# A spectral mixing layer and two MLPs on one core: Fourier phases staggered on every queue, transfers reordered

## The chip, the cores and the metric

The kernel runs on one core of a Trainium2 chip. A core has TensorE (PE: matmuls, weight loads shown as PEld), VectorE (DVE), ScalarE (ACT), GpSimd (POOL) and SyncE (SP), each with its own queue of instructions worked off in order, and 16 DMA engines, to which here SP and ACT issue. PE writes its results to PSUM, from which DVE and ACT read them. The metric is the device time of one execution in microseconds (us).

## The reference

```python
def _attn_ref(x, w_r, w_i, b_r, b_i):          # x: (2, 3008, 256)
    X = np.fft.rfft(x, axis=1)
    Yr = Xr @ w_r - Xi @ w_i + b_r
    Yi = Xr @ w_i + Xi @ w_r + b_i
    Yr = np.sign(Yr) * np.maximum(np.abs(Yr) - 0.01, 0.0)      # Yi alike
    return np.fft.irfft(Yr + 1j * Yi, n=3008, axis=1)

x = attn_out.reshape(6016, 256)
h = x @ w_in                                   # (256, 2048), float64 weights
x = (np.maximum(h, 0.0) + alpha * np.minimum(h, 0.0)) @ w_out
h = x @ w_in2
g = where(h >= 1, h, where(h <= -1, 0, (h + 1) ** 2 / 4))
return g @ w_out2
```

## The kernel before

The sequence of 3008 points is a product of 47 and 64. The Fourier transform is done in two matmul stages with a trip through DRAM between them, the inverse likewise.

- `f1` (L216): one of 16 x groups (8 for each of the two batches), the 47-point stage: 4 fp32 matmuls (the trace counts 8), results copied from two PSUM tiles by ACT (L224) and DVE (L226) to `ae`, stored to `a_dr` in two halves (`store_a`), and read back transposed (`load_a`) into `a_sb`.
- The second stage runs over 24 items (12 pairs of frequencies for each batch). For an item j, `f2` (L296) makes the spectrum (`psf`), ACT writes its rounded part fh (L305) and a negated third of it (L307), DVE the remainder fl (L306). `mix` (L310) first lets ACT negate a third of fl (L312); then PE runs 26 matmuls with the complex weights `wm` (L316, L321 to L323; L323 reads fl), and DVE applies the threshold (clip L326, y L327). `split_y` splits y into yh (ACT, L334) and yl (POOL, L335). `i1` (L338) is the 64-point inverse stage, 6 matmuls to `psi`, copied by ACT to ve (L346) and stored to `v_dr`.
- `p3` (L360) is the 47-point inverse stage for one of 16 groups: loads of v from `v_dr`, 8 matmuls (L367; 16 in the trace), copied by ACT (L371) and DVE (L373) to `y`.
- The MLPs run over 2 layers, 12 chunks of up to 512 rows and 16 blocks f of 128 hidden units: `first` (matmuls to `psh`, L421 and L422 on DVE make ta), `late` (gh on ACT L405, gl on POOL or, for odd f of the first chunk, DVE, L406) and `second` three steps behind.
- The float64 weights are split into two float32 parts on the core: `convert_w` in four parts over ACT (L143, L144, L159), DVE (L145, L171, L156, L161) and POOL (L162, L164, L165); the buffers cm and cp are two deep. The generator `conversions` gives one step at each `next(conv, None)`: a light step (parts 3 and 1, and two DMA issues on ACT for a weight block two ahead) and a heavy one (parts 2 and 0) take turns, 35 in all for the first layer.

The order on each queue is the order in which the code is written (a manual schedule). One turn of the loop (L461 to L487) writes, for item j: f2 of j + 2, an f1 of batch 1 (j < 5), split_y of j - 1, mix of j, some transfers, split_n (j < 6; it splits the constants of the inverse stage), p3 from j = 16, i1 of j - 2 with its copy, and a conversion step. PSUM has two tags, h and o, with four buffers each. The p3 of batch 1 stand in the second MLP chunk.

Of the kernel before, what the change touches and what calls it, by code (L numbers as in the profile page):

```python
# [79 lines left out]
def spectral_mlp_kernel(ctx: ExitStack, tc: tile.TileContext, x, w_r, w_i, bias, c_e, c_f1, c_f2,  # L80
# [159 lines left out]
    def load_m(k):  # L240
        nc.sync.dma_start(m_t[k].rearrange("p k f -> p (k f)"), c_f2[:, 1024 * k:1024 * (k + 1)])
# [54 lines left out]
    def f2(b, i):  # L296
        ps = psum.tile([128, 4, 128], F32, tag="h", name=f"psf{b}_{i}")
        for k in range(2):
            for c in range(2):
# [4 lines left out]
        xl = piece([128, 4, 192], F32R, f"fl{b}_{i}")
        A.activation(xh[:, :, 64:192], ps, AF.Copy)  # L305
        V.tensor_tensor(xl[:, :, 64:192], ps, xh[:, :, 64:192].bitcast(F32), op=ALU.subtract)  # L306
        A.mul(xh[:, :, 0:64], xh[:, :, 128:192].bitcast(F32), -1.0)  # L307
        xt[b, i] = xh, xl

    def mix(b, i):  # L310
        xh, xl = xt.pop((b, i))
        A.mul(xl[:, :, 0:64], xl[:, :, 128:192].bitcast(F32), -1.0)  # L312
        ps = psum.tile([128, 2, D], F32, tag="o", name=f"psm{b}_{i}")
        for k in range(2):
            o = ps[:, k, :]
            T.matmul(o, e_t, b_t, start=True, stop=False)  # L316
            for c in range(2):
                j = 2 * k + c
                for r, off in ((0, 64), (1, 0)):
# [40 lines left out]
    def p3(g):  # L360
# [36 lines left out]
    def late(step):  # L397

        if step is None:
            return  # L400
        l, c, f = step
        ps, gh, gl, ta, tb = gt[step]
        if l == 1:
            V.tensor_tensor(ta, ps, tb, op=ALU.max)  # L404
        A.activation(gh, ta, AF.Copy)  # L405
        (V if (l, c) == (0, 0) and f % 2 else G).tensor_tensor(gl, ta, gh.bitcast(F32), op=ALU.subtract)  # L406

    def first(l, c, f, before):
# [81 lines left out]
    DEPTH = 3  # L490
    seq = [(l, c, f) for l in range(2) for c in range(NC) for f in range(NF)]
    for i in range(len(seq) + DEPTH):
        if i < len(seq):
# [57 lines left out]
```

## Time and profile before

| | us |
|---|---|
| median of 3 runs (lowest, highest) | 1300.51 (1299.91, 1305.77) |
| the profiled execution | 1304.99 |
| its span, first to last instruction | 1303.2 |
| PE busy | 1235.4 (95%) |
| DVE, ACT, POOL busy | 702.3, 528.7, 656.8 |

The share of busy PE time is an average over a Fourier part of some 235 us and the MLPs behind it. A matmul's end is modelled, so its start, and the start of the next, say more than its length. The rows that the prediction uses stand below.

### The profile page before, as it was taken

Reading aid. Unit: us, or ns where it says so; the run is one execution under the profiler, and the core shown is the slowest. Engines: PE = TensorE matmul, PEld = TensorE weight load, DVE = VectorE, ACT = ScalarE, POOL = GpSimd, SP = SyncE. Lnnn points to the kernel's source line nnn. Section 1 sums busy time; section 2 is a strip of 40 time slices with the busy share of each in tenths; the row PEclk is TensorE's granted clock in tenths of the full one; section 3 lists DMA queues with packets and bytes.
Section 4 is the critical chain, followed back from the end, with each engine's and each line's share of the span. In section 5 each row is a group of like instructions: output and inputs, shape, how many; then the busy total and the mean of one; then the engine's idle time right before and its main releaser. Section 6 shows DMA issues by size and latency. Waiting matters only on the chain.

```text
span 1303.2 us, 16032 instructions
## 1 busy us (share of the span) xinstructions
PE 1235.4 (95%) x5958; PEld 1046.6 (80%) x5958; DVE 702.3 (54%) x1034; ACT 528.7 (41%) x905; POOL 656.8 (50%) x512
## 2 busy tenths in 40 slices
PE   8687777979999999999999999999999999999998
PEld 6676777758888889888888898888888988888887
DVE  1443334885566666655555576455545554555453
ACT  1344444433233333332222235454544454445544
POOL 0014533773577777765444468444444444444444
PEclk8898999989999999999999999999999999999999
DMA  9953333503001010000000010000000000000000
GB/s 264 303 169 114 89 114 89 145 17 97 18 17 33 17 33 17 18 1 1 1 1 1 1 65 1 17 17 1 17 17 17 1 15 17 17 1 17 17 17 15
DMA packets 37181, 59.38 MB, mean 46 GB/s; under 512 B 3248, under 2 KB 25328, under 8 KB 37104
## 3 DMA queue, kind: packets, MB, share of 16 engines
q1 hardware_dynamic: 22016, 39.08, 9.3%
q10 hardware_dynamic: 15088, 19.28, 5.0%
q8 instruction: 46, 0.75, 0.2%
q14 instruction: 31, 0.25, 0.1%
HBM read 39.61 MB, written 18.74 MB: 45 GB/s over the span
## 4 chain that ended last, share of the span: by engine, by line
PE 87%; ACT 4%; DVE 3%; DMA 3%; POOL 1%; issue 1%; ACTq 1%; SPq 0%; DVEq 0%; POOLq 0%
PE psh L99 13%; PE psh L100 13%; PE pso L100 13%; PE psh L101 13%; PE pso L99 13%; PE pso L101 13%; PE ps L367 2%; PE psm L323 2%; PE psm L322 2%; PE psm L321 2%; DMA x<-in_x 1%; PE ps L222 1%; ACT yh L334 1%; ACT fh L305 1%; DMA a_dr<-ae 1%
## 5 line engine op out<-in xcount | busy, mean ns | idle before, releaser
L406 POOL TENSOR_TENSOR gl<-ta,gh 128x512 fp32r<-128x512 f32 (+1 forms) x376 | 485.0, 1292 | 444.6 <-ACT gh L405 443.6
L405 ACT ACTIVATE gh<-ta 128x512 fp32r<-128x512 f32 (+1 forms) x384 | 239.0, 622 | 310.5 <-DVE ta L422 302.4
L100 PE MATMUL pso<-gl,w 128*128 128x512 f32 (+1 forms) x768 | 299.1, 389 | 7.0 <-DVE gl L406 5.5
L99 PE MATMUL psh<-mxh,w 128*128 128x512 f32 (+1 forms) x768 | 297.9, 388 | 4.1 <-POOL w L165 4.1
L100 PE MATMUL psh<-mxl,w 128*128 128x512 f32 (+1 forms) x768 | 297.6, 388 | 0.0
L99 PE MATMUL pso<-gh,w 128*128 128x512 f32 (+1 forms) x768 | 297.2, 387 | 0.0
L101 PE MATMUL pso<-gh,w 128*128 128x512 f32 (+1 forms) x768 | 296.6, 386 | 0.0
L101 PE MATMUL psh<-mxh,w 128*128 128x512 f32 (+1 forms) x768 | 296.3, 386 | 0.0
L425 DVE TENSOR_SCALAR tb<-psh 128x512 f32<-128x512 f32 (+1 forms) x192 | 130.4, 679 | 233.9 <-PE psh L101 232.7
L421 DVE TENSOR_SCALAR tb<-psh,alpha_t 128x512 f32<-128x512 f32 (+1 forms) x192 | 141.6, 738 | 160.1 <-PE psh L101 159.9
L426 ACT ACTIVATE tb<-tb 128x512 f32<-128x512 f32 (+1 forms) x192 | 119.8, 624 | 262.2 <-DVE tb L425 262.2
L100 PEld LDWEIGHTS pso<-gl,w 128*128 128x128 f32 x768 | 144.7, 188 | 38.2 <-DVE gl L406 7.6
L99 PEld LDWEIGHTS psh<-mxh,w 128*128 128x128 f32 x768 | 144.6, 188 | 33.1 <-POOL w L165 5.0
L99 PEld LDWEIGHTS pso<-gh,w 128*128 128x128 f32 x768 | 144.6, 188 | 28.3
L101 PEld LDWEIGHTS psh<-mxh,w 128*128 128x128 f32 x768 | 144.4, 188 | 28.0
L101 PEld LDWEIGHTS pso<-gh,w 128*128 128x128 f32 x768 | 144.6, 188 | 27.5
L100 PEld LDWEIGHTS psh<-mxl,w 128*128 128x128 f32 x768 | 144.6, 188 | 26.7
L422 DVE SCALAR_TENSOR_TENSOR ta<-psh,tb 128x512 f32<-128x512 f32 (+1 forms) x192 | 130.7, 681 | 20.5 <-POOL gl L406 1.5
L404 DVE TENSOR_TENSOR ta<-psh,tb 128x512 f32<-128x512 f32 (+1 forms) x192 | 128.4, 669 | 0.2 <-ACT tb L426 0.2
L335 POOL TENSOR_TENSOR yl<-y,yh 128x512 fp32r<-128x512 f32 x24 | 31.1, 1297 | 135.2 <-ACT yh L334 119.0
L323 PE MATMUL psm<-wm,fl 128*128 128x256 f32 x192 | 60.4, 314 | 39.5 <-ACT fl L312 39.4
L323 PEld LDWEIGHTS psm<-wm,fl 128*128 128x128 f32 x192 | 40.4, 210 | 44.1 <-ACT fl L312 44.1
(62 smaller groups left out, 1017.8 us busy)
## 6 DMA issues: line engine op xcount, KB each, us to landing
u<-in_w_in ACTq DMA_DIRECT2D x32, 256.0 KB, 3.0
u<-in_w_out ACTq DMA_DIRECT2D x32, 256.0 KB, 3.5
a_dr<-ae SPq DMA_DIRECT2D x32, 192.0 KB, 4.5
v_dr<-ve SPq DMA_DIRECT2D x12, 512.0 KB, 4.7
v<-v_dr SPq DMA_DIRECT2D x16, 384.0 KB, 3.9
x<-in_x SPq DMA_DIRECT2D x15, 384.0 KB, 7.4
out<-yt SPq DMA_DIRECT2D x20, 256.0 KB, 2.1
a<-a_dr SPq DMA_DIRECT2D x6, 768.0 KB, 7.6
```

Of the source, the lines that this page charges most:

```text
L99: T.matmul(ps, wl, xh, start=start, stop=False)
L100: T.matmul(ps, wh, xl, start=False, stop=False)
L101: T.matmul(ps, wh, xh, start=False, stop=stop)
L323: T.matmul(o, xl[:, j, off:off + 128], wm[r][:, 0, c, :], start=False, stop=last)
L335: G.tensor_tensor(yl, y32, yh.bitcast(F32), op=ALU.subtract)
L404: V.tensor_tensor(ta, ps, tb, op=ALU.max)
L405: A.activation(gh, ta, AF.Copy)
L406: (V if (l, c) == (0, 0) and f % 2 else G).tensor_tensor(gl, ta, gh.bitcast(F32), op=ALU.subtract)
L421: V.tensor_scalar(tb, ps, 0.0, alpha_t[:, f:f + 1], op0=ALU.min, op1=ALU.mult)
L422: V.scalar_tensor_tensor(ta, ps, 0.0, tb, op0=ALU.max, op1=ALU.add)
L425: V.tensor_scalar(tb, ps, 1.0, -1.0, op0=ALU.min, op1=ALU.max)
L426: A.activation(tb, tb, AF.Square, bias=0.5, scale=0.5)
```

## The change

The change moves instructions and transfers; the arithmetic and the number of instructions stay the same on each engine.

- In an item's turn of the loop the negation of fl is a function of its own (`negate_low`) and is written for item j + 1; the threshold (`threshold`) of item j - 1 comes behind the f2 of j + 2 and right ahead of split_y; the copy of i1 (`evict_i1`) comes one turn later, behind split_y; p3 comes ahead of the mix.
- f1 and p3 take both PSUM tiles from tag h.
- Conversion steps begin at item 5 (before: 3), and even items from 10 on take two: 26 steps in the items, before 21.
- The p3 of batch 1 move from the second MLP chunk to steps 8 to 15 of the first. In layer 0, late() works on the step's own block, not on the one before.
- Transfers: m is loaded in halves, the constants n one by one from SP (before: all three on ACT, early), w_r and w_i from SP behind x group 9 (before: early on ACT), x groups 8 to 15 and the pieces of a in another order.

```diff
@@ -217,7 +217,7 @@
-            ps = psum.tile([96, 2, D], F32, tag="h" if i else "o", name=f"ps1_{b}_{j}_{i}")
+            ps = psum.tile([96, 2, D], F32, tag="h", name=f"ps1_{b}_{j}_{i}")
...
-    load_m(0)
-    wm32 = [rot.tile([128, 2, D], F32, tag="tb", name=f"wm32_{k}") for k in range(2)]
-    A.dma_start(wm32[0], w_r.rearrange("(c p) e -> p c e", p=128))
-    A.dma_start(wm32[1], w_i.rearrange("(c p) e -> p c e", p=128))
...
-        if g in (3, 5, 7):
-            load_x(8 + (g - 3) // 2)
+        if g == 5:
+            load_m(0, 0)
+        if g == 6:
+            load_x(8)
     load_a(0, A_PARTS[:2])
+    load_x(9)
+    for k, w in enumerate((w_r, w_i)):
+        nc.sync.dma_start(wm32[k], w.rearrange("(c p) e -> p c e", p=128))
     for g in range(8):
         store_a(g, 1)
+    load_x(10)
+    load_m(0, 1)
     load_a(0, A_PARTS[2:3])
-    load_x(11)
-    load_m(1)
-    load_a(0, A_PARTS[3:])
-    load_x(12)
     f1(8)
-    load_x(13)
     f1(9)
-    n32 = [rot.tile([128, 8, 128], F32, tag="wst", bufs=3, name=f"n32_{k}") for k in range(3)]
-    for k in range(3):
-        A.dma_start(n32[k].rearrange("p k f -> p (k f)"), c_i1[:, 1024 * k:1024 * (k + 1)])
...
         A.activation(xh[:, :, 64:192], ps, AF.Copy)
+        A.mul(xh[:, :, 0:64], xh[:, :, 128:192].bitcast(F32), -1.0)
         V.tensor_tensor(xl[:, :, 64:192], ps, xh[:, :, 64:192].bitcast(F32), op=ALU.subtract)
-        A.mul(xh[:, :, 0:64], xh[:, :, 128:192].bitcast(F32), -1.0)
         xt[b, i] = xh, xl
+
+    def negate_low(b, i):
+        xl = xt[b, i][1]
+        A.mul(xl[:, :, 0:64], xl[:, :, 128:192].bitcast(F32), -1.0)
...
-        late(before)
+        late((l, c, f) if l == 0 else before if before[0] == 1 else None)
...
     f1(10)
-    load_x(14)
-    for g in range(8, 11):
-        store_a(g, 0)
-        store_a(g, 1)
-    load_x(15)
     f2(*items[1])
+    negate_low(*items[0])
+    for k, g in ((0, 11), (1, 12)):
+        store_a(8 + k, 0)
+        store_a(8 + k, 1)
+        load_x(g)
+    load_a(0, A_PARTS[3:4])
+    load_n(0)
+    store_a(10, 0)
+    store_a(10, 1)
+    load_m(1, 0)
     for j in range(n):
         if j + 2 < n:
             f2(*items[j + 2])
+        if j >= 1:
+            threshold(*items[j - 1])
+            split_y(*items[j - 1])
+        if j >= 3:
+            evict_i1(*items[j - 3])
+        if j + 1 < n:
+            negate_low(*items[j + 1])
         if j < 5:
             f1(11 + j)
-        if j >= 1:
-            split_y(*items[j - 1])
+        if 14 <= j < 17:
+            load_v(j - 14)
+        if j >= 16:
+            p3(j - 16)
         mix(*items[j])
...
-        if j >= 3:
+        if j >= 5:
             next(conv, None)
+        if j >= 10 and j % 2 == 0:
+            next(conv, None)
...
-        if (l, c) == (0, 1) and i < len(seq) and f % 2 == 1:
-            p3(8 + f // 2)
+        if (l, c) == (0, 0) and f >= 8:
+            p3(f)
```

ACT's queue in the turn of item 8 of batch 0. Names as above; the first number in a name is the item. Before:

```order
L305 ACTIVATE fh_10_830<-psf_10_825 128x4x128
L307 ACTIVATE fh_10_830<-fh_10_830 128x4x64
L334 ACTIVATE yh_7_835<-y_0_7_805 128x512
L312 ACTIVATE fl_8_703<-fl_8_703 128x4x64
L346 ACTIVATE ve_6_879<-psi_6_872 128x512
L159 ACTIVATE w_1_881<-cm_1_757 128x512
L143 ACTIVATE cm_2_885<-u_2_694 128x512
L144 ACTIVATE u_2_694<-u_2_694 128x512
```

After:

```order
L307 ACTIVATE fh_10_812<-psf_10_807 128x4x128
L308 ACTIVATE fh_10_812<-fh_10_812 128x4x64
L343 ACTIVATE yh_7_821<-y_0_7_818 128x512
L358 ACTIVATE ve_4_764<-psi_5_795 128x512
L314 ACTIVATE fl_9_752<-fl_9_752 128x4x64
L159 ACTIVATE w_0_863<-cm_0_741 128x512
L143 ACTIVATE cm_1_867<-u_1_682 128x512
L144 ACTIVATE u_1_682<-u_1_682 128x512
```

The negation in this turn is that of item 9, not 8, and the copy to ve that of the inverse of item 5, not 6.

DVE's queue in the same turn. Before:

```order
L306 TENSOR_TENSOR fl_10_831<-psf_10_825,fh_10_830 128x4x128
L326 TENSOR_SCALAR clip_8_867<-psm_8_840 128x512
L327 TENSOR_TENSOR y_0_8_868<-psm_8_840,clip_8_867 128x512
L161 TENSOR_SCALAR cp_1_758<-cm_1_757 128x512
L145 TENSOR_SCALAR cp_2_886<-u_2_694 128x512
```

After:

```order
L309 TENSOR_TENSOR fl_10_813<-psf_10_807,fh_10_812 128x4x128
L335 TENSOR_SCALAR clip_7_817<-psm_7_767 128x512
L336 TENSOR_TENSOR y_0_7_818<-psm_7_767,clip_7_817 128x512
L161 TENSOR_SCALAR cp_0_742<-cm_0_741 128x512
L145 TENSOR_SCALAR cp_1_868<-u_1_682 128x512
```

Between the two fl the threshold is now that of the item before, whose y the yh of the same turn reads.

DVE's queue in the first MLP chunk, steps 6 and 7. Before:

```order
L421 TENSOR_SCALAR tb_0_6_2128<-psh_0_6_2118,alpha_t 128x512
L422 SCALAR_TENSOR_TENSOR ta_0_6_2127<-psh_0_6_2118,tb_0_6_2128 128x512
L406 TENSOR_TENSOR gl_0_5_2098<-ta_0_5_2099,gh_0_5_2097 128x512
L161 TENSOR_SCALAR cp_12_2080<-cm_12_2079 128x512
L145 TENSOR_SCALAR cp_13_2138<-u_13_2049 128x512
L421 TENSOR_SCALAR tb_0_7_2158<-psh_0_7_2148,alpha_t 128x512
L422 SCALAR_TENSOR_TENSOR ta_0_7_2157<-psh_0_7_2148,tb_0_7_2158 128x512
L171 TENSOR_SCALAR cm_13_2137<-cm_13_2137 128x512
L156 SCALAR_TENSOR_TENSOR cm_13_2137<-cm_13_2137,cp_13_2138 128x512
```

After:

```order
L432 TENSOR_SCALAR tb_0_6_2171<-psh_0_6_2161,alpha_t 128x512
L433 SCALAR_TENSOR_TENSOR ta_0_6_2170<-psh_0_6_2161,tb_0_6_2171 128x512
L171 TENSOR_SCALAR cm_15_2150<-cm_15_2150 128x512
L156 SCALAR_TENSOR_TENSOR cm_15_2150<-cm_15_2150,cp_15_2151 128x512
L432 TENSOR_SCALAR tb_0_7_2196<-psh_0_7_2186,alpha_t 128x512
L433 SCALAR_TENSOR_TENSOR ta_0_7_2195<-psh_0_7_2186,tb_0_7_2196 128x512
L417 TENSOR_TENSOR gl_0_7_2194<-ta_0_7_2195,gh_0_7_2193 128x512
L161 TENSOR_SCALAR cp_15_2151<-cm_15_2150 128x512
```

An odd step's gl stands in the step itself, behind its ta, and the conversions are two to three weight blocks further on.

## Rows read from the trace of the kernel before

**Rows 1.** The page's slices: busy tenths of PE in 40 equal slices.
```profile
PE   8687777979999999999999999999999999999998
```
**Rows 2.** PE's waits, 60:233: who waited for whom; total us, times, longest.
```profile
PE psm L323 <- ACT fl L312: 39.4, 20, 3.0
```
**Rows 3.** Timeline, ACT and DVE, 121:131: start, length, instruction [idle before].
```profile
121.24 0.48 ACTq L133 DMA_DIRECT2D u<-in_w_out  x1
...
127.55 0.63 ACT L159 ACTIVATE w<-cm 128x512 fp32r<-128x512 f32 x1
...
129.19 0.58 ACT L305 ACTIVATE fh<-psf 128x512 fp32r<-128x512 f32 x1
129.80 0.69 DVE L306 TENSOR_TENSOR fl<-psf,fh 128x512 fp32r<-128x512 f32 x1 [1.29 <-ACT fh L305]
130.12 0.61 ACT L334 ACTIVATE yh<-y 128x512 fp32r<-128x512 f32 x1
130.64 0.40 ACT L312 ACTIVATE fl<-fl 128x256 fp32r<-128x256 f32 x1
```
**Rows 4.** Timeline, DVE: clips of items 0, 4 and 23, and y of 23.
```profile
52.92 0.69 DVE L326 TENSOR_SCALAR clip<-psm 128x512 f32<-128x512 f32 x1 [3.23 <-PE psm L323]
...
79.71 0.69 DVE L326 TENSOR_SCALAR clip<-psm 128x512 f32<-128x512 f32 x1 [3.15 <-PE psm L323]
...
232.41 0.69 DVE L326 TENSOR_SCALAR clip<-psm 128x512 f32<-128x512 f32 x1 [6.76 <-PE psm L323]
233.20 0.69 DVE L327 TENSOR_TENSOR y<-psm,clip 128x512 f32<-128x512 f32 x1
```
**Rows 5.** Timeline, PE: one item with a p3.
```profile
199.15 1.05 PE L300 MATMUL psf<-m,a 128*128 128x128 f32 x8
199.96 0.36 PE L316 MATMUL psm<-b_t,e_t 128*128 128x256 f32 x1
...
202.28 0.38 PE L323 MATMUL psm<-wm,fl 128*128 128x256 f32 x1 [1.37 <-ACT fl L312]
...
204.74 1.95 PE L367 MATMUL ps<-g,v 96*128 96x128 f32 x16
206.45 0.36 PE L99 MATMUL psi<-yh,n 128*128 128x256 f32 x1
```
**Rows 6.** Start: PE timeline (four f1; group 11); window (PE, PEld, DVE, ACT, POOL; PEclk, DMA share, GB/s).
```profile
14.62 7.12 PE L222 MATMUL ps<-x,c 96*96 96x256 f32 x32 [0.35 <-DMA x<-in_x]
...
45.26 3.70 PE L222 MATMUL ps<-x,c 96*96 96x256 f32 x8 [10.04 <-DMA x<-in_x]
...
20.00:40.00 20.00, 13.39 (x57) 9.47 (x55) 7.60 (x14) 6.03 (x12) 0.00 (x0) 0.83 0.98 327
```
**Rows 7.** Timeline, POOL and ACT: a conversion operation; a wait for POOL's L165.
```profile
132.05 1.29 POOL L164 TENSOR_TENSOR cm<-cm,w 128x512 f32<-128x512 f32 x1
...
244.52 0.68 ACT L143 ACTIVATE cm<-u 128x512 f32<-128x512 f32 x1 [1.90 <-POOL w L165]
```
**Rows 8.** The page's DMA issues: count, KB each, us to landing.
```profile
v_dr<-ve SPq DMA_DIRECT2D x12, 512.0 KB, 4.7
v<-v_dr SPq DMA_DIRECT2D x16, 384.0 KB, 3.9
```
**Rows 9.** Timeline, DVE: first step of chunks 0, 1, 2 (L421); two L171.
```profile
236.37 0.75 DVE L421 TENSOR_SCALAR tb<-psh,alpha_t 128x512 f32<-128x512 f32 x1 [0.57 <-PE psh L101]
...
239.84 0.42 DVE L171 TENSOR_SCALAR cm<-cm 128x512 f32<-128x512 f32 x1
...
254.13 1.40 DVE L171 TENSOR_SCALAR cm<-cm 128x512 f32<-128x512 f32 x1
...
294.79 0.75 DVE L421 TENSOR_SCALAR tb<-psh,alpha_t 128x512 f32<-128x512 f32 x1 [2.32 <-PE psh L101]
...
352.86 0.75 DVE L421 TENSOR_SCALAR tb<-psh,alpha_t 128x512 f32<-128x512 f32 x1 [0.83 <-PE psh L101]
```
**Rows 10.** Window over most items with p3, columns as in rows 6.
```profile
162.00:233.00 71.00, 55.90 (x424) 54.28 (x423) 27.52 (x47) 28.01 (x56) 26.33 (x21) 0.92 0.31 93
```

More of the change, by code (lines that the diff above doesn't have):

```diff
@@ L238, in store_a, with load_m @@
         nc.sync.dma_start(a_dr[b][h][4 * j:4 * j + 4].rearrange("t p f -> p t f"), aes[g][48 * h:48 * h + 48])
-    def load_m(k):
-        nc.sync.dma_start(m_t[k].rearrange("p k f -> p (k f)"), c_f2[:, 1024 * k:1024 * (k + 1)])
+    def load_m(k, half):
+        nc.sync.dma_start(m_t[k][:, 4 * half:4 * half + 4, :].rearrange("p k f -> p (k f)"),
+                          c_f2[:, 1024 * k + 512 * half:1024 * k + 512 * half + 512])
     for g in range(8):
@@ L257, in spectral_mlp_kernel @@
     A.dma_start(b32, bias)
+    A.dma_start(alpha_t, alpha)
+    wm32 = [rot.tile([128, 2, D], F32, tag="tb", name=f"wm32_{k}") for k in range(2)]
     for g in range(8):
@@ L285, in spectral_mlp_kernel, with load_n @@
         V.tensor_tensor(b_t[p:p + 32, :], b32[p:p + 32, :], b_t[p:p + 32, :].bitcast(F32), op=ALU.subtract)
+    n32 = [rot.tile([128, 8, 128], F32, tag="wst", bufs=3, name=f"n32_{k}") for k in range(3)]
+    def load_n(k):
+        nc.sync.dma_start(n32[k].rearrange("p k f -> p (k f)"), c_i1[:, 1024 * k:1024 * (k + 1)])
     n_h = []
@@ L323, in mix, with threshold @@
                     T.matmul(o, xl[:, j, off:off + 128], wm[r][:, 0, c, :], start=False, stop=last)
+        y_32[b, i] = ps
+    def threshold(b, i):
+        ps = y_32[b, i]
         cl_ = rot.tile([128, 2, D], F32, tag="ta", name=f"clip{b}_{i}")
@@ L339, in i1 @@
         yh, yl = yt.pop((b, i))
-        ps = psum.tile([128, 2, D], F32, tag="o", name=f"psi{b}_{i}")
+        ps = yt[b, i] = psum.tile([128, 2, D], F32, tag="o", name=f"psi{b}_{i}")
         for k in range(2):
@@ L343, in i1, with evict_i1 @@
             mm3(ps[:, k, :], n_h[q][:, 0, r, :], n_h[q][:, 1, r, :], yh[:, k, :], yl[:, k, :], True, True)
+    def evict_i1(b, i):
+        ps = yt.pop((b, i))
         if i % 2 == 0:
@@ L363, in p3 @@
             y[b] = block(f"a{b}", [128, 2, S], F32, f"yt{b}")
-        ps = [psum.tile([128, 4, 128], F32, tag="ho"[c], name=f"ps3_{b}_{j}_{c}") for c in range(2)]
+        ps = [psum.tile([128, 4, 128], F32, tag="h", name=f"ps3_{b}_{j}_{c}") for c in range(2)]
         for c in range(2):
@@ L397, in late @@
     def late(step):
[L399 to L406, printed above, removed]
+        if step is not None:
+            l, c, f = step
+            ps, gh, gl, ta, tb = gt[step]
+            if l == 1:
+                V.tensor_tensor(ta, ps, tb, op=ALU.max)
+            A.activation(gh, ta, AF.Copy)
+            (V if (l, c) == (0, 0) and f % 2 else G).tensor_tensor(gl, ta, gh.bitcast(F32), op=ALU.subtract)
     def first(l, c, f, before):
@@ L463, in spectral_mlp_kernel @@
             f2(*items[j + 2])
+        if j >= 1:
[5 more added lines that the diff above has]
+            negate_low(*items[j + 1])
         if j < 5:
             f1(11 + j)
-        if j >= 1:
-            split_y(*items[j - 1])
+        if 14 <= j < 17:
+            load_v(j - 14)
+        if j >= 16:
+            p3(j - 16)
         mix(*items[j])
+        if j < 3:
+            load_x(13 + j)
         if j < 5:
@@ L471, in spectral_mlp_kernel @@
             store_a(11 + j, 1)
-        if j == 2:
-            load_m(2)
+        if j == 0:
+            load_a(0, A_PARTS[4:])
+            load_m(1, 1)
+        if j == 1:
+            load_n(1)
+        if j == 3:
+            load_m(2, 0)
+            load_n(2)
+        if j == 5:
+            load_m(2, 1)
         if 5 <= j < 10:
@@ L485, in spectral_mlp_kernel @@
             i1(*items[j - 2])
-        if j >= 3:
+        if j >= 5:
             next(conv, None)
+        if j >= 10 and j % 2 == 0:
+            next(conv, None)
+    threshold(*items[n - 1])
     split_y(*items[n - 1])
+    evict_i1(*items[n - 3])
     DEPTH = 3
@@ L505, in spectral_mlp_kernel @@
                 i1(*items[n - 2 + i])
-            if i == 1:
+            if 1 <= i < 3:
+                evict_i1(*items[n - 3 + i])
+            if i == 2:
                 for g in range(8, 8 + len(v_tags[1])):
```

6 lines of the change are left out of this document (removed).

## The prediction

> **What bounds the kernel now.** I read the page's slices first: the reader is to see that TensorE (PE) is at 9 tenths from the tenth slice of 32.6 us on, and at 6 to 8 in eight of the nine before it [rows 1]. So only the first 300 us or so can give much. Next, who PE waits for there: between 60 and 233 us there is one name, the matmul L323 of the mix, behind ScalarE's (ACT) negation L312, 39.4 us in 20 waits [rows 2]. Third, the order of one item, to see why L312 is late: ACT first splits the spectrum of the item two ahead (fh), then yh, then negates, and only afterwards copies the inverse transform (ve) and converts weights [rows 3]. A mix waits for a negation that stands behind a split, the split behind weight conversion, the conversion behind ve, and ve behind the inverse matmuls that follow the mix: a ring around two engines, once per item. Item 4's clip starts at 79.71 us and item 23's at 232.41 [rows 4]: 152.7 us for 19 items, 8.0 each. PE's own work for one item is far less [rows 5]: f2 0.81 (199.15 to 199.96), mix 26 matmuls of 0.117 (21 of them fill 202.28 to 204.74), 3.05; i1 6 of 0.117, 0.70; together 4.56, and 6.27 with the 1.71 of a p3 (204.74 to 206.45). Before 50 us the bound is DMA: PE waits 10.04 us for x group 11 [rows 6], in a stretch whose DMA engines are 98% busy at 327 GB/s.
>
> **The change, part by part.** Every sum is made on the profiled execution (1304.99 us); its difference is then taken off the median, 1300.51.
>
> (1) DMA order. I count the bytes that stand ahead of x group 11 on both queues. Before: 12 x groups of 0.393 MB, 16 stores of 0.197, m 0.524, w_r and w_i 0.524, the a pieces 0 to 11, 1.57, n 1.573, small constants 0.29: 12.35 MB. After: n has gone behind it, half an m in place of a whole one is no saving because both halves are ahead, and two stores of group 8 have come ahead: 11.17 MB. The difference of 1.18 MB at 327 GB/s is 3.6 us, so group 11 starts PE at 41.65 instead of 45.26. From there to item 0's clip I keep the old 7.66 us (45.26 to 52.92, the row of the clip of item 0 [rows 4]), slow matmuls included (3.70 for this group's eight against 7.12 for 32 earlier on [rows 6]), since PE comes out of a wait here again: 49.3. Items 1 to 4 carry an f1 each, 1.78 us (7.12 for four groups [rows 6]); PE alone needs 0.81 + 1.78 + 3.05 = 5.64, and 0.70 more from item 3 on: 23.96 us. The DMA just keeps up: group 15, the last, has 6.3 MB ahead of it behind group 11, 19 us at that rate, and is wanted some 25 us later. Item 4's clip: 73.3 against 79.71, **-6.4 us**. What is late next there is n (0.524 MB ahead of split_n 0, which holds ACT and VectorE, DVE); it lands before ACT's turn for item 2, with some 5 us to spare.
>
> (2) The ring is opened. L312 now stands in the item before its mix, so a mix finds it done; ve is copied one item later; clip and y (L326, L327) have moved behind fl on DVE. What takes the place of the ring is a smaller loop of ACT and DVE alone, because yh now stands behind fh, fl, clip and y of the same item. Its length, start to start [rows 3, 4]: fh to fl 0.61, fl 0.69, clip to y 0.79, y to yh 0.70 (y's length), yh to the next 0.52, ve as much, being a copy of the same size, negation 0.40: 4.2 us. The fl to clip and y to yh steps are not shown by the trace of before, since there the next operation was never queued directly; they lie between these lengths and 0.1 more for a hand-over. Weight conversion comes on top: its heavy step 1.64 (127.55 to 129.19), its light step two DMA issues of about 0.48, half of it hidden under the operation ahead, 0.5. So 5.85 or 4.7, and 6.35 in every second item from 10 on, which takes both. Where the light step is ahead of the heavy one (item 12 in this stretch), the heavy step's L143 needs the buffer that L165 on GpSimd (POOL) gives back in the same item: yl, L164, L165 of 1.3 each (one of them [rows 7]) after yh's 0.61, then 1.1 of ACT work, so 8.3. Such a wait is in the trace, 1.90 us [rows 7]. Items 5 to 13: 6.6 (four DMA issues and a split_n) + 5.3 + 4.7 + 5.85 + 4.7 + 6.35 + 5.85 + 8.3 + 4.7 = 52.35. All of them exceed PE's 4.56, two by little, so the loop sets the end, with PE waiting a little at each mix. From item 4's mix to the loop's first negation 5.8; item 13's period ends 58.2 us after item 4's mix.
>
> Now v: the copy of item 11's ve comes one item later than before, and the load of v for p3(0) stands right behind its store. Store 4.7 and load 3.9 [rows 8] end 8.4 us later, p3 takes 1.71, so mix 16 starts at 10.1, some 3.7 us after its negation. From there each item costs PE 6.27; ACT's loop is 5.1 to 8.3 with 0.4 for p3's copy, about 6.8 in the mean, but it has that wait to catch up, so I take PE: 3.05 + 5 x 6.27 + 2 x 5.46 (the last two have no f2) = 45.3. Sum: 58.2 + 10.1 + 45.3 = 113.6 against 152.7, **-39.1 us**.
>
> (3) To the first MLP step. Before, 3.96 us from the last clip to the first L421 [rows 4, 9], of which one p3, 1.71, now stands ahead of the mix (and is in the sum above): **-1.7 us**.
>
> (4) The first two MLP chunks. Before: 58.4 and 58.1 us (236.37, 294.79, 352.86 [rows 9]). In the second of them PE works through, 8 p3 included, so PE's own time for a chunk is 58.1 - 13.7 = 44.4. In the first, DVE's conversions set the pace over most steps. After, 26 in place of 21 conversion steps lie in the items, so the conversions end with step 8; p3 moves to steps 8 to 15 of the first chunk. First half: 29.2 if DVE's pace stays, 22.2 if PE sets it; second half 22.2 + 13.7; second chunk 44.4. With the old pace 109.5 against 116.5, **-7 us**; to PE's own, -14. The new place of late() costs on this stretch: on odd steps gl on DVE now waits for gh of the same step, about 0.8 each (a copy of yh's size, 0.61 [rows 3], and two hand-overs) for 4 steps, which leaves -3.8. I take -7, the old pace, as the nearest row. Elsewhere in layer 0 late() moves work that PE's matmuls cover.
>
> (5) Two charges. The granted clock averaged 0.92 in 162 to 233 [rows 10]; the levels are 1.2 and 2.4 GHz, so 16% of the time was at the lower one. PE is now the bound there: 8% of some 55 us, **+4**; nought if it stays high, 9 if it falls twice as often. And DVE's L171 took 0.42 in one place and 1.40 in another, where POOL was at work [rows 9]. In items 10 to 23 ten weight blocks go through L171 and L156; with L156 priced alike, at +0.98 each that is at most 19.6 us, at least 0 (ACT's 0.5 to 1.6 of conversion runs beside them). I take **+4**.
>
> The Trainium skill bears on this (SBUF — State Buffer, Who interferes with whom): VectorE in its two-port modes, or with two SBUF inputs, and GpSimd exclude one another for whole instructions, and whichever starts second waits. The pair of L171 durations agrees. By that rule alone, with every such pair of operations colliding, the charge would be 19.6 instead of 4, which is the first rival.
>
> Sum: -6.4 - 39.1 - 1.7 - 7 + 4 + 4 = -46.2. On the median: 1300.5 - 46.2 = **1254 us**.
>
> **The rivals.** *DVE and POOL collide in each denser item*: the conversions hold fl of the next item up. For it: the 1.40 [rows 9], and four POOL operations of 1.3 in an item that takes both steps. Against: fl, clip and y themselves read PSUM and keep 0.69 in every row shown, beside POOL or not. It puts 19.6 for 4, and -3.8 for -7: 1273.
> *The loop is slack and PE alone sets the items*: 10 x 4.56 in place of 58.2, -12.6, and no charge for collisions: 1238. Against it: yh really does stand behind fl, clip and y.
> *The wait only moves*: negations come no earlier, because ACT's queue as a whole is late; items 5 to 23 keep 8.0, and only the start, the step to the MLP and the MLP chunks gain 15, less the charges of 8: 1293, in half of these cases within 0.5% of before.
> *Slower: the clock stays at 1.2 GHz through the items*, since PE still pauses at each mix. PE's own 10 x 4.56 + 7 x 6.27 + 2 x 5.46 = 100.4 us would become 200.8 against 152.7, +48 less 15: about 1334. It decides from two thirds of the time at the lower level on (100.4 x 1.67 = 168 eats all gains); the trace shows 16%.
>
> **How the numbers follow.** Forecast 0.62, collisions 0.18, PE alone 0.09, the wait moves 0.07 (half of it 0.035 within 0.5%), clock 0.04. Range: the low end is the sum without charges and with PE's pace in the first chunk (-54.2 - 7 = -61), 1239; the high end has 19.6, 9 and -3.8 (-22), 1278. It leaves out the slower case, the moved wait and some of both neighbours: 0.2. A measurement of this kernel tells 0.5% (6.5 us) from no change. Faster by more than that: 0.62 + 0.18 + 0.09 + 0.035, 0.93; within 0.03; slower 0.04.
>
> **What would show it.** Right: L312's successor gone from PE's waits in the items; clips 5.5 to 6.3 us apart; yh or POOL's L165 as releasers on ACT and PE; group 11 near 41.7 us; first MLP step near 190. Wrong: clips still 7 to 8 us apart (the wait moved), a granted clock of 0.7 or less over the items, a p3 that waits longer than 4 us for v, or the first chunk still 58 us long.

## The result and the profile after

The changed kernel takes 1252.98 us (median; 1252.85 to 1253.21), the kernel before 1300.49 us in the same comparison: ratio 0.9626, 95% interval 0.9601 to 0.9651. The forecast was 1254.0. The profiled execution of after took 1252.99 us (span 1251.2), that of before 1304.99, so between the two traces 52.0 us have to be found; 4.5 us of that lie in the profiled execution of before, which was that much above its median.

The page's slices, PE's row, and PE's waits from 50 to 192 us (who waited for whom: total us, times, longest). They answer [rows 1, 2]:

```profile
PE   6998998999999999999999999999999999999998
```

```profile
PE psm L321 <- DVE y L336: 5.4, 3, 2.7
PE psm L328 <- ACT fl L314: 1.5, 4, 0.5
...
PE ps L379 <- DMA v<-v_dr: 0.5, 1, 0.5
```

The 39.4 us behind ScalarE's negation are 1.5. L314 is the old L312. PE is at 9 tenths from the eighth slice on, and was so from the tenth.

The clips of items 4 and 23 and the first step of chunks 0, 1 and 2 in after's DVE timeline (start, length, instruction), against [rows 4, 9]; L335 is the old L326, L432 the old L421:

```profile
75.49 0.68 DVE L335 TENSOR_SCALAR clip<-psm 128x512 f32<-128x512 f32 x1
...
191.45 0.69 DVE L335 TENSOR_SCALAR clip<-psm 128x512 f32<-128x512 f32 x1
...
192.78 0.74 DVE L432 TENSOR_SCALAR tb<-psh,alpha_t 128x512 f32<-128x512 f32 x1
...
257.26 0.75 DVE L432 TENSOR_SCALAR tb<-psh,alpha_t 128x512 f32<-128x512 f32 x1 [0.83 <-PE psh L101]
...
300.86 0.75 DVE L432 TENSOR_SCALAR tb<-psh,alpha_t 128x512 f32<-128x512 f32 x1 [1.17 <-PE psh L101]
```

Chunk 2 begins 52.0 us earlier (352.86 to 300.86): the whole difference lies ahead of it. The same marks were read in the trace of every kernel below (the names are those of the experiments). The stages in us, each a difference of two such starts:

| kernel | median | to item 4's clip | items 4 to 23 | to the first MLP step | chunks 0, 1 | chunk 2 begins |
|---|---|---|---|---|---|---|
| before | 1300.49 | 79.7 | 152.7 | 4.0 | 116.5 | 352.9 |
| after | 1252.98 | 75.5 | 116.0 | 1.3 | 108.1 | 300.9 |
| loop_only | 1257.99 | 81.5 | 103.7 | 2.2 | 117.8 | 305.1 |
| old_dma | 1258.80 | 81.2 | 116.0 | 1.3 | 108.4 | 306.9 |
| old_mlp | 1255.11 | 75.5 | 116.0 | 1.3 | 110.4 | 303.2 |
| single | 1254.24 | 78.2 | 107.8 | 2.2 | 113.9 | 302.1 |
| neg_only | 1251.04 | 79.7 | 99.5 | 4.3 | 117.6 | 301.0 |
| neg_back | 1332.61 | 85.8 | 178.9 | 2.2 | 108.4 | 375.3 |
| single_p17 | 1246.98 | 78.0 | 100.1 | 2.2 | 115.2 | 295.4 |
| extra_p17 | 1241.47 | 76.1 | 103.2 | 1.3 | 108.3 | 289.0 |
| old_order | 1243.39 | 74.5 | 105.5 | 3.0 | 109.5 | 292.4 |
| best | 1240.08 | 74.3 | 100.8 | 3.0 | 107.8 | 285.9 |

Two things in the row of after ask for an explanation. Its items take 116.0 us, 12 to 16 us more than in several kernels that contain only a part of the change. And it is one time for a bundle of edits, which does not say which edit did it.

### The profile page after: what moved, and what is told of

Read it like the earlier page. It is cut to its first block, busy times and chain, and to the rows that moved or that the text cites. A ratio compares the mean times of both kernels' runs of the same rounds, so it can differ in the third digit from the quotient of the medians.

```text
span 1251.2 us, 16024 instructions
## 1 busy us (share of the span) xinstructions
PE 1220.5 (98%) x5958; PEld 1038.1 (83%) x5958; DVE 714.9 (57%) x1034; ACT 527.8 (42%) x905; POOL 655.8 (52%) x512
## 3 DMA queue, kind: packets, MB, share of 16 engines
q1 hardware_dynamic: 23424, 41.18, 10.4%
## 4 chain that ended last, share of the span: by engine, by line
PE 86%; DVE 5%; ACT 2%; POOL 2%; DMA 2%; issue 1%; SPq 0%; ACTq 0%; POOLq 0%; DVEq 0%
PE pso L100 13%; PE psh L100 13%; PE psh L99 13%; PE pso L99 13%; PE pso L101 13%; PE psh L101 13%; PE ps L222 2%; DMA x<-in_x 1%; PE ps L379 1%; DVE cm L156 1%; DMA a_dr<-ae 1%; PE psm L326 1%; PE psm L328 1%; PE psm L327 1%; PE psf L302 1%
## 5 line engine op out<-in xcount | busy, mean ns | idle before, releaser
L417 POOL TENSOR_TENSOR gl<-ta,gh 128x512 fp32r<-128x512 f32 (+1 forms) x376 | 478.6, 1274 | 473.0 <-ACT gh L416 457.0
L432 DVE TENSOR_SCALAR tb<-psh,alpha_t 128x512 f32<-128x512 f32 (+1 forms) x192 | 141.6, 737 | 153.7 <-PE psh L101 153.7
L100 PEld LDWEIGHTS pso<-gl,w 128*128 128x128 f32 x768 | 144.2, 188 | 29.3 <-POOL gl L417 2.7
L96 DVE TENSOR_TENSOR mxl<-yt,mxh 128x1024 fp32r<-128x1024 f32 (+1 forms) x24 | 37.7, 1570 | 39.2 <-ACT mxh L93 39.2
L328 PE MATMUL psm<-wm,fl 128*128 128x256 f32 x192 | 56.3, 293 | 1.5 <-ACT fl L314 1.5
```

Source lines behind the costliest of these rows:

```text
L96: V.tensor_tensor(lo, src, hi.bitcast(F32), op=ALU.subtract)
L100: T.matmul(ps, wh, xl, start=False, stop=False)
L432: V.tensor_scalar(tb, ps, 0.0, alpha_t[:, f:f + 1], op0=ALU.min, op1=ALU.mult)
```

## Which edit carries the gain

**The whole new order inside an item, alone (loop_only).** Transfers, conversion steps (one per item from item 3), third phase and `late()` as before; in the loop:

```
+        if j >= 1:
+            threshold(*items[j - 1])
+            split_y(*items[j - 1])
+        if j >= 3:
+            evict_i1(*items[j - 3])
+        if j + 1 < n:
+            negate_low(*items[j + 1])
...
-        if j >= 1:
-            split_y(*items[j - 1])
         mix(*items[j])
```

> The new order inside an item alone (negation, threshold, copy of i1, place of p3, PSUM tags), with the transfers, the conversion steps (one per item from item 3), late() and the p3 of batch 1 as in the kernel before. Theory: the order carries nearly all of the gain, and single steps even let the items run at PE's pace: 150 us between the clips of items 4 and 23 become 103 to 108, start and MLP as before: 1246 to 1254. Rival: the parts add up and the order in the items is only the 34 us by which these items shrank: 1264 to 1268.

Measured: 1257.99 us, ratio 0.9655 [0.9641, 0.9670], between the two ranges. The items take 103.7 us, as the theory has it; the start and the chunks do not gain. So some 43 of the 47.5 us come with the order inside the items, as the prediction's step (2) has it.

**One line of it (neg_only).** The kernel before with the negation moved and nothing else:

```
+    def negate_low(b, i):
+        xl = xt[b, i][1]
+        A.mul(xl[:, :, 0:64], xl[:, :, 128:192].bitcast(F32), -1.0)
...
     def mix(b, i):
         xh, xl = xt.pop((b, i))
-        A.mul(xl[:, :, 0:64], xl[:, :, 128:192].bitcast(F32), -1.0)
...
+    negate_low(*items[0])
     for j in range(n):
         if j + 2 < n:
             f2(*items[j + 2])
+        if j + 1 < n:
+            negate_low(*items[j + 1])
```

> The kernel before with one line moved: the negation of the low part's copy is written one item earlier, ahead of the next item's f2, instead of directly ahead of its own mix; everything else is as before. Theory (the wait of PE on ScalarE's fl, 39.4 us over 20 items, is this line and nothing else): nearly all of the gain of the run with the whole new order in the items, 1258 us there, so 1256 to 1264, and the stretch from item 4's clip to item 23's near 104 us where it was 152.7. Rival (the wait needs the moved line and the new places of the conversion steps together, since ScalarE stays behind them): 1275 to 1290, with PE's wait on fl at 0.8 us per item or more.

Measured: 1251.04 us (1250.26 to 1253.19), ratio 0.9612 [0.9591, 0.9634]: less than forecast by the theory, and no slower than the whole change. Neg_only's window from 80 to 175 us (length; busy us and instructions of PE, PEld, DVE, ACT, POOL; granted clock; DMA share; GB/s), and the clips of items 4 and 23:

```profile
80.00:175.00 95.00, 95.00 (x820) 95.00 (x820) 69.19 (x98) 61.20 (x123) 58.68 (x42) 1.00 0.56 175
```

```profile
79.66 0.69 DVE L329 TENSOR_SCALAR clip<-psm 128x512 f32<-128x512 f32 x1 [1.41 <-PE psm L326]
...
179.14 0.69 DVE L329 TENSOR_SCALAR clip<-psm 128x512 f32<-128x512 f32 x1 [1.90 <-PE psm L326]
```

PE is busy for 95.00 of 95.00 us at the full clock, and each clip waits for PE's last matmul of the mix (L326 there), as it should where PE is the bound. The items take 99.5 us in place of 152.7. All that the rest of the change gains and loses against this kernel cancels by the table: 4.2 us at the start (transfers), 3.0 at the step to the MLP, 9.5 in the chunks, against 16.5 us that after's items take longer.

**The line put back into the changed kernel (neg_back).**

```
-    negate_low(*items[0])
...
-        if j + 1 < n:
-            negate_low(*items[j + 1])
...
+        negate_low(*items[j])
         mix(*items[j])
```

> The changed kernel with that one line put back directly ahead of its own mix; DMA order, conversion steps, late writing of the first layer and the third phase's place stay as changed. Theory: PE waits again near 2.0 us for fl in each item, 20 x 2.0 = 39 us, less what the shorter conversion steps spare, so 1280 to 1294. Rival (the other places of the new order have taken ScalarE's queue off the path by themselves): under 1265.

Measured: 1332.61 us, ratio 1.0229 [1.0199, 1.0259]: slower than before, and far past what the theory allowed. PE's waits from 50 to 235 us, and one item in the timeline of ACT, DVE and PE:

```profile
PE psm L328 <- ACT fl L314: 55.4, 19, 3.6
```

```profile
114.32 0.68 DVE L335 TENSOR_SCALAR clip<-psm 128x512 f32<-128x512 f32 x1
115.10 0.69 DVE L336 TENSOR_TENSOR y<-psm,clip 128x512 f32<-128x512 f32 x1
115.83 0.63 ACT L343 ACTIVATE yh<-y 128x512 fp32r<-128x512 f32 x1 [1.70 <-DVE y L336]
116.36 0.58 ACT L358 ACTIVATE ve<-psi 128x512 f32<-128x512 f32 x1
116.84 0.41 ACT L314 ACTIVATE fl<-fl 128x256 fp32r<-128x256 f32 x1
117.30 0.58 PE L328 MATMUL psm<-wm,fl 128*128 128x256 f32 x1 [3.55 <-ACT fl L314]
...
120.24 0.42 PE L328 MATMUL psm<-wm,fl 128*128 128x256 f32 x1
...
121.16 0.28 PE L328 MATMUL psm<-wm,fl 128*128 128x256 f32 x1
...
122.00 1.06 PE L302 MATMUL psf<-m,a 128*128 128x128 f32 x8
123.09 0.60 ACT L307 ACTIVATE fh<-psf 128x512 fp32r<-128x512 f32 x1 [4.17 <-PE psf L302]
123.72 0.69 DVE L309 TENSOR_TENSOR fl<-psf,fh 128x512 fp32r<-128x512 f32 x1 [7.26 <-ACT fh L307]
124.33 0.68 DVE L335 TENSOR_SCALAR clip<-psm 128x512 f32<-128x512 f32 x1
```

From clip to clip 10.0 us, and every link waits for the one above it: y, yh, ve, negation, then the rest of the mix, i1 and f2 on PE, and only then fh and fl, behind which the next clip now stands, although its mix ended at 121.4. Before, clip stood directly behind its mix and did not wait for the f2 that PE runs behind that mix. So by these rows the moved clip lengthens the ring, and the moved negation is what opens it. The rows show one thing more: after this wait of 3.55 us PE's matmuls take 0.42 where they take 0.28 later; the granted clock of the window from 80 to 175 us is 0.86 in this kernel, against 1.00 in neg_only.

## What the transfers and the MLP's edits carry

**Transfers as before (old_dma)**, else as after:

```
-        if g == 5:
-            load_m(0, 0)
-        if g == 6:
-            load_x(8)
+        if g in (3, 5, 7):
+            load_x(8 + (g - 3) // 2)
...
+    for k in range(3):
+        A.dma_start(n32[k].rearrange("p k f -> p (k f)"), c_i1[:, 1024 * k:1024 * (k + 1)])
```

> The kernel after with all transfers of the start and the items in the order and on the queues of the kernel before (m still in two pieces, one behind the other). Theory: the first mix starts 4 to 5 us later and items 1 to 4 lose 2 more: 1257 to 1261. Rival: the order of the transfers buys nothing, since items 5 to 23 are paced by ACT, DVE and POOL anyway and make the start good: 1252 to 1254.

Measured: 1258.80 us, ratio 0.9662 [0.9646, 0.9677]: 5.8 us are the transfers' part, as the theory has it. Item 4's clip comes 5.7 us later, and all later stages keep their lengths, so it is a plain shift.

**`late()` and the third phase of batch 1 as before (old_mlp)**:

```
-        late((l, c, f) if l == 0 else before if before[0] == 1 else None)
+        late(before)
...
-        if (l, c) == (0, 0) and f >= 8:
-            p3(f)
+        if (l, c) == (0, 1) and i < len(seq) and f % 2 == 1:
+            p3(8 + f // 2)
```

> The kernel after with late() and the p3 of batch 1 (second MLP chunk) as in the kernel before. Theory: the 8 us of the first two chunks come from the conversion steps that left them, not from the place of p3, since p3's matmuls are PE's work in either chunk: first chunk 50 to 52, second 58, total 1252 to 1256. Rival: p3 filled time in which PE waited: 1259 to 1262.

Measured: 1255.11 us, ratio 0.9636 [0.9622, 0.9650]. The two chunks take 110.4 us (52.4 and 58.1, as the theory has it) where after has 108.1: some 2 us. The rest of the chunks' gain (117.8 in loop_only, with 21 conversion steps in the items, to 110.4 here, with 26) is that of the conversion steps.

## Why after's items are long

**No doubled steps (single).**

```
-        if j >= 5:
-            next(conv, None)
-        if j >= 10 and j % 2 == 0:
+        if j >= 4:
             next(conv, None)
```

> The kernel after, with one conversion step per item from item 4 on and no second step in the even items from 10 (20 steps in the items in place of 26). Theory: the second step is what holds items 10 to 23 (POOL and DVE work on the path between two splits), and what is left over is hidden under the p3 in steps 8 to 14 of the first MLP chunk. Then the clips of items 9 to 23 span 79 us in place of 92.2, the first chunk stays near 64, and the time is 1240 to 1243. Rival: conversion work only moves, what the items save the first chunk pays: 1250 to 1255, first chunk 75 or more.

Measured: 1254.24 us, ratio 0.9625 [0.9609, 0.9641], 0.1% from after: the theory's time is missed by 11 us. Items 9 to 15 take 29.1 us (39.4 in after), but it is taken back: 2.7 us up to item 4's clip (1.7 of it in item 4, which now has a step), 2.0 in the items up to 9, 0.9 at the step to the MLP and 5.8 in the chunks. And items 15 to 23, with four steps fewer, take 53.0 us where after takes 52.8, because of one place. Single's clips of items 15 and 16 (DVE), and PE's first p3:

```profile
132.99 0.68 DVE L335 TENSOR_SCALAR clip<-psm 128x512 f32<-128x512 f32 x1
145.42 0.68 DVE L335 TENSOR_SCALAR clip<-psm 128x512 f32<-128x512 f32 x1
```

```profile
134.26 3.79 PE L379 MATMUL ps<-g,v 96*128 96x128 f32 x16 [3.84 <-DMA v<-v_dr]
```

The wait for v, 3.84 us, is the 3.7 that the prediction puts at mix 16. In after it is 0.5, since the longer items cover it. After the wait the p3 itself takes 3.79 instead of 1.95, the double; the granted clock is 0.53 from 134 to 138 us, 0.61 from there to 142 and 1.00 in the next four. The clips stand 12.4 us apart.

**The third phase one item later (single_p17).**

```
-        if j >= 16:
-            p3(j - 16)
+        if j >= 17:
+            p3(j - 17)
+        if j == n - 1:
+            p3(7)
```

> One conversion step per item from item 4 on, none doubled, as in the run single (1254), and the third phase of the first batch one item later, with two of its pieces in the last item. Theory: what single lost between items 15 and 16 (12.4 us for one clip to the next, 6 us over its neighbours) is the wait for v's round trip through DRAM, and one item more covers it: items 15 to 23 in 47 to 48 us where single had 53.0, the first chunk's second half still near 41.6, the whole near 1248. Rival (the 12.4 us is the work of the first item of the mixed stretch, not a wait): the long clip moves to item 17 and the whole stays at 1253 to 1255.

Measured: 1246.98 us, ratio 0.9579 [0.9559, 0.9598]. Items 15 to 23 take 45.8 us (53.0 in single). The wait for v is gone, and with it the slow matmuls behind it: a wait of 3.84 us had cost 7.

**Three doubled steps, among the p3 (extra_p17)**: single_p17 with

```
-        if j >= 4:
+        if j >= 5:
             next(conv, None)
+        if j in (16, 19, 22):
+            next(conv, None)
```

> As single_p17 but with doubled conversion steps at items 16, 19 and 22 alone, so that the first chunk finds its weights almost as early as in the changed kernel, and the steps from item 5 on. Theory: items 9 to 15 keep 29 us (39.4 in the changed kernel), items 15 to 23 take 47 to 49, the first chunk's second half 37 to 39 (35.2 and 41.6 in the changed kernel and in single): 1253 - 10 - 2 + 3 = near 1243, and under both kernels. Rival (the time of the steps only moves: what a doubled step costs in a mixed item is what it spares in the chunk): 1248 to 1251, as single_p17.

Measured: 1241.47 us (1239.04 to 1242.45), ratio 0.9534 [0.9507, 0.9560]. With 22 steps in the items the chunks take 108.3 us, as with after's 26 (108.1), where 20 steps leave 115.2: the four further doubled steps of after bought nothing. The rival (what a step costs in a mixed item it spares in the chunk) falls: +3.1 us in the items, -6.9 in the chunks (and -1.9 at the start, where item 4 has no step again).

**GpSimd relieved (pool_less)**: after without

```
-            G.tensor_tensor(p, p, low, op=ALU.mult)
...
-            G.tensor_tensor(m, m, wt[l, f][:, 0, :].bitcast(F32), op=ALU.subtract)
```

> The changed kernel without two of GpSimd's operations on each weight tile (the low part's scaling and the subtraction of the rounded part), so the weights' low halves are left out of the output; every operation of VectorE and ScalarE stays. Theory (doubled items 10 to 15 are long because GpSimd's work is slow and slows VectorE's beside it: 1.16, 1.51, 1.38 and 1.68 us where the same four take 0.42, 0.42, 0.42 and 0.69 alone): items 9 to 15 fall from 39.4 to 31 to 34 us. Rival (ScalarE's and VectorE's own work of two steps makes these items long): 37 us or more.

Measured in a single execution: 1240.40 us; items 9 to 15 take 35.2 us, between the two, and items 4 to 23 109.2 (116.0 in after). Neither theory nor rival holds by itself: what GpSimd no longer does was worth 4.2 of the 39.4 us. After, 99.26 to 138.62 (six items), ACT's waits, the longest of DVE and PE, and the window's row (columns as above):

```profile
ACT yh L343 <- DVE y L336: 10.4, 6, 1.9
ACT fh L307 <- POOL cp L162: 3.1, 2, 1.5
ACT cm L143 <- POOL w L165: 3.1, 1, 3.1
DVE fl L309 <- ACT fh L307: 8.0, 5, 3.0
PE psm L321 <- DVE y L336: 4.1, 2, 2.7
```

```profile
99.26:138.62 39.36, 34.15 (x260) 33.14 (x259) 29.12 (x38) 22.59 (x45) 28.55 (x21) 0.91 0.39 126
```

ACT is busy for 22.59 us and waits 10.4 + 3.1 + 3.1: 39.2 of 39.36. That sum alone names no bound, for PE's closes as well (busy 34.15, waits of 4.1, 0.6 and 0.5: 39.35). The names of the waits say more: ACT waits for DVE's y, DVE's fl for ACT's fh, and both for GpSimd. The chain of work that ended last, followed back by the profile, runs from 98.9 to 119.0 us mostly over GpSimd (yl, L162, L164, L165), and from there over ACT and DVE, with L171 and L156 of the doubled item in it. So it is a ring of ACT and DVE, with GpSimd's conversions in its way, and not one queue. In pool_less ACT waits 11.1 us for y and 1.7 for L165: the wait behind L162 is gone, the one for y stays. It comes with the new order: in each of the six items ACT stands 1.7 us at yh, which is now next in its queue, until fl, clip and y of the same item are through DVE.

**The order inside the items as before, save the negation (old_order).** The changed kernel with clip and y back behind their mix, ve behind its i1, `split_y` ahead of `mix`, p3 behind it:

```
         y_32[b, i] = ps
+        threshold(b, i)
...
-        if j >= 1:
-            threshold(*items[j - 1])
-            split_y(*items[j - 1])
-        if j >= 3:
-            evict_i1(*items[j - 3])
         if j + 1 < n:
             negate_low(*items[j + 1])
...
+        if j >= 1:
+            split_y(*items[j - 1])
         mix(*items[j])
```

> The changed kernel with the order inside an item as before the change (threshold right behind its mix, eviction of i1 right behind i1, splitting of y ahead of mix, third phase behind mix) and of the new order only the negation one item earlier. DMA order, doubled conversion steps, late writing and chunks stay as changed. Theory (what the new order adds to the moved negation costs time, since clip then stands behind f2's evictions and VectorE's conversion operations run beside GpSimd's subtraction for y: 1251 against 1258 in the two runs without the other changes): items 9 to 15 fall from 39.4 to 30 to 35 us, the whole 1241 to 1248. Rival (with doubled steps it is the amount of work, not its place, that makes items 9 to 15 long): 38 to 40 there and 1250 to 1254 in all.

Measured: 1243.39 us, ratio 0.9551 [0.9529, 0.9572]. Items 9 to 15 take 32.9 us. The time is the theory's; of its two reasons, the one on VectorE's operations beside GpSimd's does not hold. Four conversion operations of VectorE in one doubled item of after, with GpSimd's beside them, and in one of old_order:

```profile
126.69 1.16 DVE L161 TENSOR_SCALAR cp<-cm 128x512 uint32<-128x512 uint32 x1
...
127.53 1.48 POOL L344 TENSOR_TENSOR yl<-y,yh 128x512 fp32r<-128x512 f32 x1
127.78 1.51 DVE L145 TENSOR_SCALAR cp<-u 128x512 uint32<-128x512 uint32 x1
...
128.97 1.50 POOL L162 TENSOR_TENSOR cp<-cp,u 128x512 f32<-128x512 f32 x1
...
129.37 1.38 DVE L171 TENSOR_SCALAR cm<-cm 128x512 f32<-128x512 f32 x1
...
130.78 1.68 DVE L156 SCALAR_TENSOR_TENSOR cm<-cm,cp 128x512 uint32<-128x512 uint32 x1
...
131.45 0.60 ACT L307 ACTIVATE fh<-psf 128x512 fp32r<-128x512 f32 x1 [1.54 <-POOL cp L162]
```

```profile
104.38 0.42 DVE L161 TENSOR_SCALAR cp<-cm 128x512 uint32<-128x512 uint32 x1
104.71 0.42 DVE L145 TENSOR_SCALAR cp<-u 128x512 uint32<-128x512 uint32 x1
105.05 1.53 DVE L171 TENSOR_SCALAR cm<-cm 128x512 f32<-128x512 f32 x1
106.61 1.67 DVE L156 SCALAR_TENSOR_TENSOR cm<-cm,cp 128x512 uint32<-128x512 uint32 x1
```

In old_order L171 and L156 stay as slow, and the 18 such operations of the six items sum to 19.8 us there, to 18.3 in after. The collisions are not fewer. What is gone is ACT's 1.7 us at yh: no wait of yh for y is left there, and ACT's largest is 3.5 us for f2. How much of the 6.5 us is that wait, and how much GpSimd's work on the path, no run separates.

**Both together (best)**: old_order with the doubled steps of extra_p17.

> As old_order, with doubled conversion steps at items 16, 19 and 22 alone. Theory: item 0's clip as changed (51.5), items 4 to 23 at TensorE's own pace as in the run with the negation alone (99.5 us where extra_p17 has 103.2), chunks as in extra_p17 (108.3): 1241.5 - 4 + 1 = near 1238. Rival (the doubled steps cost in this order what they cost in the other, and the transition to the first chunk comes back to the 4.3 us of the run with the negation alone): 1241 to 1244.

Measured: 1240.08 us (1238.46 to 1241.69), ratio 0.9529 [0.9508, 0.9549]. The items take 100.8 us, 2.4 less than in extra_p17, and the step to the MLP 1.7 more, so it lies between theory and rival; from extra_p17 the times don't tell it. Both are some 12 us under the changed kernel. With single steps in items 9 to 15, best takes 28.0 us there; so all four cases are measured. The doubled steps cost 4.9 us in the old order (32.9 against 28.0) and 10.3 in the new (39.4 against 29.1); the new order costs 1.1 us with single steps and 6.5 with doubled ones. After's long items need both.

## The prediction, point by point

**Start.** Group 11 comes 1.8 us earlier, not 3.6, and mix 0 follows at once. After's PE timeline (x group 8, group 11, item 0's mix) and window 20 to 40, against [rows 6]:

```profile
23.79 3.70 PE L222 MATMUL ps<-x,c 96*96 96x256 f32 x8 [4.40 <-DMA x<-in_x]
...
43.46 1.94 PE L222 MATMUL ps<-x,c 96*96 96x256 f32 x8 [0.41 <-DMA x<-in_x]
45.05 0.47 PE L321 MATMUL psm<-b_t,e_t 128*128 128x256 f32 x1
...
48.19 0.28 PE L328 MATMUL psm<-wm,fl 128*128 128x256 f32 x1
```

```profile
20.00:40.00 20.00, 10.90 (x31) 7.39 (x32) 4.56 (x10) 3.73 (x7) 0.00 (x0) 0.61 0.89 285
```

The bytes were counted, but divided by 327 GB/s; the stretch ran at 285. Nor is one trace enough for this term: with the transfers as before, group 11 starts at 45.26 in before, but at 47.42, 46.78 and 46.95 in neg_only, loop_only and old_dma; with the new ones it starts between 43.46 and 45.28 (after, single, best, old_order). Then the old 7.66 us from group 11 to the clip were kept, since "PE comes out of a wait here again": it had waited 0.41 us, not 10.04, and its group took 1.94 us, not 3.70. The mix's last matmul started 4.7 us after 43.46. The clip gained nothing by that, for it now stands behind the next f2 and its fl:

```profile
51.04 0.68 DVE L335 TENSOR_SCALAR clip<-psm 128x512 f32<-128x512 f32 x1
```

That is 7.58 us after 43.46, so the 7.66 was met by luck. The constants n were seen landing with 5 us to spare; ACT's L93 waited 3.90 us for them, until 49.17, and the fh ahead of that fl stands behind it. Items 1 to 4 take 24.45 us against 23.96. In all the start gains 4.2 us where step (1) has 6.4. Old_dma's 5.8 is nearer to 6.4 only because its item 4 comes 1.5 us later than before's, at 81.2, with the same order of transfers.

**Items.** Forecast without the charges: 113.6 us; measured 116.0. The loop of ACT and DVE that was put together from [rows 3] is there; one item of after (ACT, its DMA issues and DVE):

```profile
94.59 0.69 DVE L309 TENSOR_TENSOR fl<-psf,fh 128x512 fp32r<-128x512 f32 x1 [2.94 <-ACT fh L307]
95.20 0.68 DVE L335 TENSOR_SCALAR clip<-psm 128x512 f32<-128x512 f32 x1
95.99 0.69 DVE L336 TENSOR_TENSOR y<-psm,clip 128x512 f32<-128x512 f32 x1
...
96.71 0.63 ACT L343 ACTIVATE yh<-y 128x512 fp32r<-128x512 f32 x1 [1.70 <-DVE y L336]
96.72 0.39 ACTq L131 DMA_DIRECT2D u<-in_w_in  x1
...
97.25 0.58 ACT L358 ACTIVATE ve<-psi 128x512 f32<-128x512 f32 x1
97.73 0.41 ACT L314 ACTIVATE fl<-fl 128x256 fp32r<-128x256 f32 x1
...
98.66 0.69 DVE L309 TENSOR_TENSOR fl<-psf,fh 128x512 fp32r<-128x512 f32 x1 [0.92 <-ACT fh L307]
```

From fl to fl 4.07 us with the light step in it (4.7 by the prediction, which gave its two DMA issues 0.5; they pass under yh and ve), and in the item ahead, with the heavy step, 5.7 (5.85). A pair takes 9.7 us, two items of PE's own 4.67 take 9.3 (23.4 us for five in neg_only): a loop that binds, by little, as forecast. Single's 29.1 us for six items is that pair, three times. Over the doubled turns the sum came out near, the parts less so: item 4's clip to item 14's 57.5 us against 58.2, with 4.7 us in the first turn (6.6 forecast) and 7.7 and 8.8 in the doubled turns 10 and 12 (6.35 and 8.3); ACT's wait for L165, on which the 8.3 rests, is there, 3.1 us. From there to item 23's it is 58.5 against 55.4, most of it because the items with a p3 take 6.6 on average (items 15 to 23, 52.8 us for eight) against PE's 6.27. In the sums of this part store 4.7 and load 3.9 make 8.6 us, not 8.4, and three turns, not two, exceed PE by little (4.7); the total does not hang on either. The wait of 3.7 us for v measured 0.5, since the items ahead of it were longer.

**The charges** of +4 and +4 are the term that was too large: the items lost 36.7 us, 39.1 stood without them and 31.1 with. Clock and collisions are in the trace all the same: the granted clock of after is 0.91 in the six items shown and 0.96 over items 4 to 23 ([rows 10] had 0.92), and the four operations of the doubled item above sum to 5.7 us where the same four take 0.42, 0.42, 0.42 and 0.69 alone. But a slow operation counts only where another engine waits for its end: the last of the four ends at 132.46, and fh, which itself had waited for GpSimd's L162, at 132.05, so fl came 0.4 us late by DVE's four; what L162 held up comes on top. On the rule of the Trainium skill that was weighed there (SBUF — State Buffer, Who interferes with whom) the rows agree that the two engines delay one another; they don't make VectorE's slowed operations the price of the items, as old_order shows with more of them and less time. GpSimd's work as a whole is a part of the price: without two of its operations for each weight tile items 4 to 23 are 6.8 us shorter (pool_less).

**Step to the MLP and chunks**: -2.6 and -8.4 against -1.7 and -7; the first chunk's halves are 29.3 and 35.2 against 29.2 and 35.9, and chunk 1 is 43.6 against 44.4. The 29.2 was half of the old chunk; before's own first half took 27.9, so that this half did not gain.

**The sum**: forecast -46.2, in the traces -52.0. On the median the 4.5 us of the profiled execution of before take most of the shortfall away, so 1254 stands nearer to 1252.98 than its working deserves: the start was forecast 2.2 us too good and the items with their charges 5.6 too dear, which work against each other.

**The rivals.** *PE alone*, 1238: its condition, a slack loop, is what neg_only and best have, and there the items do run at PE's pace; in after the loop binds. *Collisions*, 1273: the mechanism is there; GpSimd is a part of what makes the items long, not the 19.6 us. *The wait only moves*: not in after, but neg_back is that case, and dearer than was thought. *The clock*: seen behind waits, as in single and neg_back.

What the prediction did not see is inside its step (2). It took the new order as a whole and found the ring opened; it did not ask which of the moves opens it. One of them does, for 53 us of the items by itself; the others made a new loop of ACT and DVE, and the kernels that have them take 4 us more in the items with single steps (loop_only against neg_only) and 10 more with doubled ones (after against old_order).

## What to carry to other kernels

Where a wait in each round names one instruction, move that one instruction alone first, and measure: the rest of a reordering has to earn its place against that. In these runs the order in which each operation stands where its last input has just come made ACT's queue wait (yh behind y, 1.7 us an item); with yh one round behind its y, as in old_order, there was no such wait. A queue's busy time and its waits fill the stretch for every queue whose waits are all named (ACT's and PE's alike in after), so that sum does not tell which queue sets the pace; follow the names of the waits until they close a ring, and change one member of it in a run.

## What the runs showed of the hardware

A wait of PE can cost more than its length. In single the 3.84 us behind v were followed by a p3 of 3.79 us in place of 1.95 at a granted clock of 0.53, and taking the wait away gave 7.2 us. It need not: in loop_only the same p3 waits 2.04 us for v and then takes 2.05. In neg_back the matmuls take 0.42 us for part of the mix behind most waits of 3.55; behind the one that ends at 108.81 all L328 but the first take 0.28.

VectorE's four conversion operations (L161, L145, L171, L156) take 0.42, 0.42, 0.42 and 0.69 us alone, and up to 1.4, 1.5, 1.5 and 1.7 beside GpSimd, whose own go from 1.3 to between 1.5 and 1.7; clip, y and fl, which read PSUM, keep 0.68 to 0.69 in all rows shown.
